# GpSimd's maxima and masks also wait for VectorE's last listed operation on two SBUF operands, in a listed order searched anew

## The chip, the core and the metric

The kernel runs on one core of a Trainium2 chip. The metric is the device time of one execution in microseconds: 606.67 us for the kernel before, the median of 3 runs (606.17 to 608.17). The five engines of the core take their instructions in the order in which the program gives them and run beside each other; semaphores order them where data passes between them. In the profile they are PE (TensorE), DVE (VectorE), ACT (ScalarE), POOL (GpSimd) and SP (SyncE, which here only issues DMAs).

## The reference, cut to what matters

Two stages follow each other for 8 batches of 576 positions. The first is linear attention with 8 heads of 64 values:

```python
def phi(x):
    proj = x @ w_phi                                  # 64 -> 128
    proj = proj - max(abs(proj), over the 128)
    return concat([exp(proj), exp(-proj)])            # 256 features
kv = phi(k).T @ v ;  z = sum over s of phi(k)
attn = (phi(q) @ kv) / (phi(q) @ z + 1e-6)
```

The second takes the 512 values of a position as x and mixes 4 experts, of which each position uses the 2 with the largest gate. Every expert is a causal softmax attention over the 576 positions with its own weights:

```python
logits = x @ w_gate;  w = softmax over the 2 largest
scores = 0.125 * (x @ wq[e]) @ (x @ wk[e]).T, causal
a = softmax(scores);  out += mask * w * (a @ (x @ wv[e]) @ wo[e])
```

All data is float32.

## The kernel before

The work is cut into 32 pairs of heads (p) for the first stage and 8 batches of 2 expert groups (n = 0 to 15) for the second; keys lie on partitions and positions along the free dimension or the other way round, as the products need it.

*First stage.* `stream_k` projects the keys of a pair (L485), `center` takes the largest absolute value of each row (L548) and subtracts it (L551), `phi_k` takes the two exponentials on ScalarE. For 28 of the 32 pairs `key_sum` adds one half of ek to zs with an accumulating DMA that GpSimd issues (`add_to`, L318), and VectorE closes the sum with one addition in SBUF (L560); TensorE then multiplies zs with ones (L621) among the products of phi(k) and v (L610). `stream_q` projects the queries (L485). For them the largest value runs across partitions, so `phi_q` has GpSimd do a PARTITION_ALL_REDUCE of u into mx (L680, 64 of them), VectorE subtracts mx from u (L682), and ScalarE takes the exponentials. `stream_n` multiplies (L707 for the denominator, L718 for the numerator), `divide` applies the reciprocals and splits the result into a high and a low float32r part (x, L751 and L285).

*Second stage.* `stream_b` projects x to q, k and v (L281), splits q and k into two parts (ql at L791, kkl at L285) and makes the scores (L838). `evac_s` copies them to the tile s in SBUF. `mask` has GpSimd set what lies behind the diagonal to a very small number (AFFINE_SELECT, L946, 80 of them). `maxima` gathers, key block by key block, the largest score of each column on VectorE (L959), has GpSimd reduce it across partitions (PARTITION_ALL_REDUCE of top into max, L963, 16 of them), and subtracts it from the scores on VectorE (L967: for each group five operations, for 1152, 896, 640, 384 and 128 elements). `expo` takes the exponentials, `add_up` sums them over key blocks (L979), `sums` sums them over partitions with ones (L1005), `attend` multiplies by v (L1034), `evac_y` scales and splits the result (yl, L285), and `out_unit` makes the output product (L281). `gates` works out the two chosen experts per position in a row of small VectorE operations (L901 to L919).

*The order of the work.* Each of these functions is a stream that yields a `Step` for every piece of work. The string ORDER (3,100 characters) is a list made by an offline search: each character names the stream that goes on next, by its place among the streams alive. The string SIDES (520 digits) settles for each copy that ScalarE or VectorE could do which of them does it (0 ScalarE, 1 VectorE). The instructions of each engine come into the program in the order of that list, and `in_order` ties each instruction to the one before it on the same engine, so that each engine keeps it. Between different engines only the data's own dependencies order anything. The class `Plan` accounts for costs while the list is worked off: `run` for an engine's instruction, `transfer` for a DMA, with GpSimd's recent instructions (`pool`, and how long each of them keeps VectorE's two-operand work out: `blocked`) and VectorE's latest operation of that kind (`shared`). These figures drive the search; they put nothing into the program.

Of the kernel before, what the change touches and what calls it, by code (L numbers as in the profile page):

```python
# [11 lines left out]
AF = mybir.ActivationFunctionType  # L12
ALU = mybir.AluOpType
# [4 lines left out]
DM, E = 512, 4  # L18
# [35 lines left out]
KVD = 6  # L54
RATE = 2.18
TRATE = 2.4
ADD_RATE = 40.0
EXIT = 95.0
ENTRY = {'F': 102.0, 'R': 99.0, 'S': -31.0, 'C': 23.0, 'Q': 10.0}
LDW = 109.0  # L60
# [4 lines left out]
def change_cost(a, b):  # L65
# [4 lines left out]


ORDER = (
    r'41000000008BB40929DEB742BC6BD9E9I88IDD1C007000=0CDBDHBD55342BEH=GG::99=BCBEBCBFDECD2E==CDB:BB478=>0DEED546EFE='
    r'BD0=79EEE9::IID=I8F8DBH:EDE>2>ID>HB9HGI3BDB9=5=1EJHF2HJH:7:DACBFF8IHIG<B0:;;H:F@A3<549<FFGD<BE;9EEHGBEE:D6E:CF'
    r'7DF88:FD3H71?2@:F:G?;;::CAH?BBB:G;G9C9CF88AH43G0G@568=83EB>DHI10DKLHD8>A==H94HGEFA897G7CF9@B8D0CB6A@8DHC5BB?IA'
    r'>=6AI;=F2;8;:;@;>8KKG?BDA=GH=G;FA;88C@DD8DB8C=;6AAFG5G9G=A9GEEGE9BAG77DBACGF;G;HB@8E;;MDO6808803IIJJFJIAH>EF;>'
    r'D48F;;;F>CA;HHEAFFE8=E6FFE@8@A8A;;5??B>:LABGGG>@@@@@H@DF=A1::::KIBHEG:@AE>?DB:999OHKE@LKMKCCLF338LL>?B28882088'
    r'88D678>IBEIG5BFEE?>79ID==93884889@KKCLJ66L02GCIE?88JCC@77DH=?99G88=DD1GAEAAD<8259<7HKH=7@FKG238808KK<HEK8F=86D'
    r'MNJMHI<E?DFJD8=G997EH=DA=<=I<H7:=KK:HH:G:H:F<KK<EEL<J::8II;IL;MLJALHKI::DAFIMF=8?FKF@?:8A8:>:HFF8K83B2H84MO5PG'
    r':LG6RCI=@E::DJHGIH::;IF>EF>FDK@?>DIHDIB=GCDDEE;;B>88DE:>CE@=FF85<AADHAG<K<<CKCAC>FIAAAI=GJH@<?FFIDDH?DJ@C=C::H'  # L80
    r'J=FJI=E@G?:9LFCC@<KI@KK999KEEC88B;>@H?8>>>CC@CAB?F?FBEBFDA3881ICDDD?BB6;;<B?D>70072B8FECBDD88>A>89B>9A=G>8>=78'
    r'L78KEEL586;9CKCMMQCOPCHKOOKLLE<998B@30I78I9DHGJ8FGG@HE6E5EA88>?41G28AI=88II7FKE?C::::K::86:BAKJ8EIAA?C6JKCKJCG'
    r'DF4F=89FFF8F89A3<87::BGBB?D78DC2GB@1JD??FG::F5?DG?CBHK::J=LB:J?>=NGKJD:8:>IH;BED8IB>>F=C;C82CBIG=C8DBFG8D9BDD8'
    r'CD?F:::G::@=JBFOAGBIQ=BQBBFJHOC<<I<D<NEJQLJLCDEK<D99KA9I=CEA0888383BD@@>G@LFAJKEJAGCEDH@<JEIF77HD6JKI9IID9CDF7'
    r'E5F?EBCHII6D87FIIHHFG0C8B<EDA888GEE48?<>@@===G=HB08659M8KPJLLGNKMD8M98;9J;L<MILL;8H986JL6ALKGIFIGI22F@HF5:8IHI'
    r'<1GHF<E<08<888077:::DF:FIAIO:PI>?=>FNCKJGL33828K9JEJ98G87IIJEDCIK:7J8IJ8H::H@I:OQDJJL:6:;LF5NMCI8B?83OCOQOCB::'
    r'B:@SHJCMI>FMB8K=J0AII:JAAJG==LK?H;8D=>F=;:IHCECG6GD89G88F<DIHEG<:::HIHJ=J5>:JB<CS@@EBBKAKEBIIJ<<9ARI6Q@Q9B9488'
    r'8138MD7N=EF<0828FLFCOJ<FLLHK8L88MKICCCJK9@9F94LK88888M87==IJ@JD7JJ?=HF>B2EGCJI<99EFA67I9IJCMLI??H@GEF88F6H?D5E'
    r'757HHJDAFEMFFFEAGAA:E:::<:IE=AJLEL:A896KLIJE8828833019=JAHD77D??HGC8=AAGIID8GJHHI86=DH;5<K8GMBNJLL=M<<A===NNJC'
    r'3JK@088<<<<FH:;;NQIMNHINOHHK42881K08::HH8MLF?MJIMAG:EH:;EG>PG66EBKRHNL:::H:PF:OMLJG8NO@GBHGIL?GIFCH8GF:;;F=>AF'  # L90
    r'D<>:EHFD:5ELKHFEEBHF::=L=9LPC>PPFCDD<DID<;TCQBBOQJIM<<<BPK@PJDAA9<BHIJOO9M<JMEJ9JNO@P@@8KN882FG=<KLJBD88GKI8IE'
    r'D88GDEIE@G?C70EDC8GF?576JF9D4?E?IJ9D9?K>@@HGGBFHI3HFG03888821887@C>@7;;M>D=<68GC6B?EHDBB8FF?E99G95E82B>8ED>C<E'
    r'<BF7F78388IJCI8CB@B:68::<KKCIDAA@:::JFHBJCABC8FHHFCF9895BEFEEB88D7:DDIED19H9HLD;99:J9GNJ=A>B6FJ?G70=;D;QHLG1JG'
    r'NMGF9F9JCII990@2IED7HC>JC=G7I5JCG7G@CHH<DF7::4;<HEJ=F9EHH@EAB;;;EE7FE;;D;=GFCG;;8@>FE5>>>AHFIG99DCFNGLCGH9@@>E'
    r'>239CO@@@:BTCSDBIFK<B?GI=@MD8887PDEA7J7L6O67BBEAKA?HACGHIE>JI06JBB>6<CD>66B=BE6>?B43>7=:<7EF2BEB5055516C;GCF;F'
    r'D<G;FA88CDF6F6HH0CG@AC884@44CC2@4?4<8;5>@3DDB>>@>>3966331>26H69:6>C<445K242@I1?3<G?A1F1H@1<@FE1ED3;@3=31A>B85@'
    r'B;8C:33E23GF2?15@>>A61=;9C6=<<;>;6?73?3>??1::>;61008228;>8;??=0>>;=7671>;=;:8;7;833<<<449<44>>>65:42<484227445'
    r'84484?0101170=95B=52;A@07649??2=:><?@?440404FD355>:?05=;A4<65<5900480474<5<6:657::48:008:297769387477742263209'
    r'000023320110::42849::2666964800790<09;79767=7069;59:0:907887887:878:50::788651017611562006605850580==;444:9<1;'
    r'6711;17<7139=68259984455456461345111111341413585112111411;3:2=32998818810081124465454452330000>>?256028=1<<15;'  # L100
    r'32056538645204042200'
)

SIDES = (
    r'11000001001100010000100000000011000000000111000000011010000001000001110100000100000000010000000000000000000000'
    r'00000000000000000000000010000000000100000001000000000000010000001100100001000000110000001010000010000000000100'
    r'00000000001000010000100110000001000000000001001000010010010000000010010000000000000001000000000001010001001110'
    r'01000000000101000001000100000010100000000010000000010000011100000000100000000010000000001000100011001000100111'
    r'00000000001000000000001000011000000110000100000111000000000000010000000001000110'
)  # L110


# [6 lines left out]
class Plan:  # L119
# [16 lines left out]

    def clocked(self, t, cost, rows):
# [19 lines left out]
    def run(self, eng, cost, w=(), r=(), rows=128, tiling=(128, 128), port=False):  # L157
        if eng == 'PE' and tiling != self.tiling:
            cost += change_cost(self.tiling, tiling)
        if eng == 'PE':  # L160
            self.tiling = tiling
        t = self.free.get(eng, 0.0)
        for k in r:
            t = max(t, self.after(self.ready, k, eng))
        for k in w:
            t = max(t, self.after(self.last, k, eng))
        if eng == 'PE':
            cost = self.clocked(t, cost, rows)
# [12 lines left out]
        for k in w:
            self.ready[k] = self.last[k] = (end, eng)

    def transfer(self, cost, issue, w, r, eng='SP'):
# [6 lines left out]
        self.free[eng] = t + issue  # L191
        ring = int(eng == 'POOL')
        self.rings[ring] = max(self.rings[ring], t + issue + 650.0) + cost
        end = self.rings[ring] + 1150.0
        for k in r:
            if end >= self.last.get(k, (0.0, 'SP'))[0]:
                self.last[k] = (end, 'SP')
# [43 lines left out]

def in_order(tc):

    last = {}
    for i in tc.nc.cur_bb.bb.instructions:
        if i.engine in last:
            tc.add_manual_dep(i, last[i.engine].name, mybir.DependencyInfo(
                mybir.DependencyClass.NoSync, mybir.DependencyReason.DATA), reason="order")
        last[i.engine] = i


@with_exitstack
def tile_linear_attn_moe(ctx, tc, qt, kt, v, wts, out):
# [643 lines left out]
    def gates(b):  # L897
# [14 lines left out]
        yield Step('ACT')
        act(20, ex, ex, [G], [], AF.Exp)
# [245 lines left out]
```

## Time and profile before

| | before |
|---|---|
| median of 3 runs | 606.67 us (606.17 to 608.17) |
| the profiled execution, own time | 607.85 us |
| its span, first to last instruction | 605.8 us |
| mean granted TensorE clock | 0.999 of full speed |
| DMA | 67.13 MB, mean 111 GB/s |

The span is what the profile covers, from the first to the last instruction of the core; the execution's own time has what lies around it as well. In the rows below an engine is busy while one of its instructions runs. A row of groups gives a line of the program, engine and operation, tiles written and read, shape, count, busy time and the mean time of one instruction, then the time for which the engine sat idle before these instructions and what ended it. A row of the timeline gives the start, the time covered, and the instruction; neighbours of one line are merged (x2 means two instructions, and the shape shown is that of the first). Of matmuls the ends are modelled, and spans on POOL are rough.

### The profile page before, as it was taken

The numbers are of one execution on the slowest core, as the hardware profiler recorded it, in microseconds if no ns is written. First come the engines' busy times: TensorE is split into PE (matmuls) and PEld (weight loads), VectorE is DVE, ScalarE is ACT, GpSimd is POOL, SyncE is SP. The second block draws the span as 40 slices with busy tenths as digits, with TensorE's granted clock in tenths as the row PEclk, the third lists the DMA queues.
The fourth block names the chain that finished last, engine by engine and source line by source line (L and its number), as shares of the span: only waits on it lengthen the run. The fifth ranks groups of instructions, "written<-read, shape, count | busy, mean of one in ns | idle before, by whom it ended". The sixth has DMA issues, their size and how long they took to land.

```text
span 605.8 us, 19534 instructions
## 1 busy us (share of the span) xinstructions
PE 582.0 (96%) x7909; PEld 447.9 (74%) x7909; DVE 553.5 (91%) x1172; ACT 449.2 (74%) x1087; POOL 275.1 (45%) x195
## 2 busy tenths in 40 slices
PE   8998999998999999999999999998999999999986
PEld 6664788566885788767885877965888677778975
DVE  6897899999999999998989999999999989998994
ACT  3998877867796878866879668866778768675653
POOL 3754553366615554346542663316743449231420
PEclk9999999999999999999999999999999999999999
DMA  8556465650436562465535544446434542221012
GB/s 217 162 152 133 102 144 124 143 125 26 101 88 148 126 172 68 106 148 135 146 83 128 137 120 116 98 131 149 103 102 100 117 94 83 37 68 40 1 49 110
DMA packets 55369, 67.13 MB, mean 111 GB/s; under 512 B 23664, under 2 KB 31216, under 8 KB 55280
## 3 DMA queue, kind: packets, MB, share of 16 engines
q1 hardware_dynamic: 47344, 50.62, 29.1%
q0 software_dynamic: 7616, 14.68, 14.8%
q8 instruction: 62, 1.02, 0.7%
q10 hardware_dynamic: 320, 0.59, 0.4%
q14 instruction: 27, 0.22, 0.1%
HBM read 36.64 MB, written 14.55 MB: 85 GB/s over the span
## 4 chain that ended last, share of the span: by engine, by line
PE 63%; DVE 18%; DMA 7%; ACT 5%; issue 4%; POOL 2%; SPq 1%; DVEq 0%; POOLq 0%; ACTq 0%
PE ps_c L281 26%; PE ps_c L485 7%; PE ps_c L718 6%; PE ps_c L838 6%; PE ps_c L610 5%; PE ps_c L1034 5%; DMA zs<-ek 5%; PE ps_c L707 4%; DVE s L967 3%; DVE top L959 2%; ACT ek L292 1%; PE ps_c L621 1%; DVE u L682 1%; DMA q_in<-in_qt_dram 1%; DVE max L979 1%
## 5 line engine op out<-in xcount | busy, mean ns | idle before, releaser
L680 POOL PARTITION_ALL_REDUCE mx<-u x64 | 146.0, 2319 | 45.2 <-ACT u L290 22.9
L281 PE MATMUL ps_c<-x,qk 128*128 128x256 f32 (+1 forms) x768 | 106.6, 298 | 0.0
L281 PEld LDWEIGHTS ps_c<-x,qk 128*128 128x128 f32 x768 | 102.4, 189 | 4.4 <-ACT u L290 1.0
L946 POOL TENSOR_SCALAR_AFFINE_SELECT s<-s 128x256 f32<-128x256 f32 (+1 forms) x80 | 44.2, 597 | 108.7 <-ACT s L290 87.1
L963 POOL PARTITION_ALL_REDUCE max<-top x16 | 57.5, 3595 | 58.7 <-DVE top L959 28.9
L318 POOL DMA_DIRECT2D zs<-ek x28 | 34.2, 1223 | 94.4 <-ACT ek L292 65.7
L967 DVE TENSOR_TENSOR s<-s,max 128x1152 f32<-128x1152 f32 (+4 forms) x80 | 73.2, 944 | 0.0
L292 ACT ACTIVATE ek<-ek 128x1024 f32<-128x1024 f32 x64 | 67.7, 1058 | 3.6 <-DVE ek L551 2.8
L292 ACT ACTIVATE s<-s 128x1152 f32<-128x1152 f32 (+4 forms) x80 | 57.5, 741 | 10.5 <-DVE s L967 10.2
L610 PE MATMUL ps_c<-ek,v_in 128*32 128x256 f32 x1024 | 61.7, 381 | 0.5 <-ACT ek L292 0.5
L290 ACT COPY s<-ps_c 128x512 f32<-128x512 f32 (+4 forms) x129 | 48.0, 427 | 11.6 <-PE ps_c L838 11.1
L281 PE MATMUL ps_c<-yh,wo 128*128 128x256 f32 (+1 forms) x256 | 52.7, 300 | 0.0
L682 DVE TENSOR_TENSOR u<-u,mx 128x576 f32<-128x576 f32 x64 | 51.6, 816 | 0.2 <-POOL mx L680 0.2
L290 ACT COPY u<-ps_c 128x320 f32<-128x320 f32 (+1 forms) x107 | 40.1, 402 | 12.7 <-PE ps_c L485 11.9
L281 PE MATMUL ps_c<-vg,x 128*128 128x260 f32 x384 | 49.1, 285 | 0.0
L1034 PE MATMUL ps_c<-s,vs 128*32 128x320 f32 (+4 forms) x896 | 46.5, 357 | 2.0 <-DVE ql L791 2.0
L281 PEld LDWEIGHTS ps_c<-vg,x 128*128 128x128 f32 x384 | 47.1, 188 | 0.8 <-issue 0.2
L610 PEld LDWEIGHTS ps_c<-ek,v_in 128*32 128x32 f32 x1024 | 31.4, 110 | 21.8 <-issue 2.7
L292 ACT ACTIVATE mx<-u 128x576 f32<-128x576 f32 x64 | 42.9, 682 | 5.8 <-DVE u L682 5.5
L548 DVE TENSOR_REDUCE pmax<-ps_c 128x4 f32<-128x512 f32 x64 | 42.7, 680 | 2.7 <-PE ps_c L485 2.5
L485 PE MATMUL ps_c<-q_in,wf 64*128 64x256 f32 (+1 forms) x256 | 43.5, 442 | 1.1 <-DVE ek L551 1.0
L1034 PEld LDWEIGHTS ps_c<-s,vs 128*32 128x32 f32 x896 | 28.1, 110 | 21.4 <-DVE ql L791 2.3
(131 smaller groups left out, 1357.9 us busy)
## 6 DMA issues: line engine op xcount, KB each, us to landing
zs<-ek POOLq DMA_DIRECT2D x28, 512.0 KB, 6.2
out_dram<-ot SPq DMA_DIRECT2D x32, 288.0 KB, 2.2
q_in<-in_qt_dram SPq DMA_DIRECT2D x60, 144.0 KB, 4.1
k_in<-in_kt_dram SPq DMA_DIRECT2D x64, 128.0 KB, 3.7
v_in<-in_v_dram SPq DMA_DIRECT2D x32, 256.0 KB, 3.2
kvd<-kvt SPq DMA_DIRECT2D x104, 48.0 KB, 2.2
kv<-kvd SPq DMA_DIRECT2D x26, 192.0 KB, 2.8
vt_in<-in_v_dram SPq DMA_DIRECT2D x16, 128.0 KB, 3.3
```

What stands on the lines that cost most here:

```text
L281: nc.tensor.matmul(o, a, b, start=start, stop=stop, skip_group_check=True)
L290: nc.scalar.copy(o, i)
L292: nc.scalar.activation(o, i, func, **kw)
L485: nc.tensor.matmul(o, a, b, start=True, stop=True, skip_group_check=True)
L548: dve(512, [mk], [pk]).tensor_reduce(out=m[:, us], in_=src, axis=AX.X, op=ALU.max, apply_absolute_value=True)
L610: nc.tensor.matmul(o[g, 0:2], v_in[:, 4 * h + t, k:64:2], ek[:, :, 2 * TURN[t] + h, :].rearrange("p c (w f) -> p c w f", w=4), start=False ...
L680: nc.gpsimd.partition_all_reduce(M, U, 128, bass_isa.ReduceOp.absmax)
L682: dve(S, [uk], [mk], port=True).tensor_tensor(out=U, in0=U, in1=M, op=ALU.subtract)
L946: nc.gpsimd.affine_select(out=d, in_=d, pattern=[[0, 2], [1, w]], compare_op=ALU.is_ge, fill=FILL, base=0, channel_multiplier=-1)
L963: nc.gpsimd.partition_all_reduce(big.rearrange("p e s -> p (e s)"), top.rearrange("p e s -> p (e s)"), 128, bass_isa.ReduceOp.max)
L967: dve(2 * (S - 128 * j), [('d', x, j)], [('max', z)], 1.11, True).tensor_tensor(out=block(s_, j, None, rows(j)), in0=block(s_, j, None, ro ...
L1034: nc.tensor.matmul(ps[r:r + 32, q0 - s0:s1 - s0], vs[:, j, 128 * g + 64 * e + k:128 * g + 64 * e + 64:2], ss[x][:, e, o + q0:o + s1], star ...
```

## The change

Three things are changed. `in_order` gives each of GpSimd's all-reduces and masks one more dependency with a semaphore: on the last VectorE instruction that stands before it in the list and reads two operands from SBUF (or copies from SBUF); operations with an operand in PSUM (tiles named ps_) do not count. GpSimd's DMA issues and memsets get no such wait. The planner is told of that wait (`pairs`), of the measured issue time of GpSimd's DMAs, another rate and landing time, and of the port flag of five small gate operations. And ORDER and SIDES are replaced as a whole: the lengths are the same, 3,100 and 520; SIDES had 93 ones and has 76.

```diff
-ADD_RATE = 40.0
+ADD_RATE = 45.0
...
 ORDER = (
...
 SIDES = (
...
         if eng == 'DVE' and port:
             cost += self.blocked(t)
             self.shared = (t, t + cost)
+            self.pairs = t + cost
+        if eng == 'POOL' and port:
+            t = max(t, self.pairs + 215.0)
         if eng == 'POOL' and self.shared[0] < t < self.shared[1]:
             t = self.shared[1]
...
-        end = self.rings[ring] + 1150.0
+        end = self.rings[ring] + (1500.0 if ring else 1150.0)
...
 def in_order(tc):
 
-    last = {}
+    def two_from_sbuf(i):
+        names = [x.bass_ap.tensor.name for x in i.ins if hasattr(x, 'bass_ap')]
+        least = 1 if isinstance(i, mybir.InstTensorCopy) else 2
+        return len(names) >= least and not any(n.startswith('ps_') for n in names)
+
+    last, pairs = {}, None
     for i in tc.nc.cur_bb.bb.instructions:
...
         last[i.engine] = i
+        if i.engine == mybir.EngineType.DVE and two_from_sbuf(i):
+            pairs = i
+        elif pairs is not None and type(i).__name__ in ('InstPartitionAllReduce', 'InstTensorScalarAffineSelect'):
+            tc.add_manual_dep(i, pairs.name, mybir.DependencyInfo(
+                mybir.DependencyClass.Sync, mybir.DependencyReason.DATA), reason="order")
...
-    def add_to(o, i, w, r):
-        plan.transfer(o.free_size() * 128 / ADD_RATE, 1000, [w], list(r), 'POOL')
+    def add_to(o, i, w, r, issue=1220):
+        plan.transfer(o.free_size() * 128 / ADD_RATE, issue, [w], list(r), 'POOL')
...
-        dve(80, [G], []).tensor_tensor(out=ge, in0=ge, in1=tri.unsqueeze(1).to_broadcast(sh4), op=ALU.mult)
+        dve(80, [G], [], port=True).tensor_tensor(out=ge, in0=ge, in1=tri.unsqueeze(1).to_broadcast(sh4), op=ALU.mult)
```

## Rows read from the trace of the kernel before

**Rows 1.** Page, parts 1 and 4: busy us (share) xinstructions; the chain by engine.

```profile
PE 582.0 (96%) x7909; PEld 447.9 (74%) x7909; DVE 553.5 (91%) x1172; ACT 449.2 (74%) x1087; POOL 275.1 (45%) x195
...
PE 63%; DVE 18%; DMA 7%; ACT 5%; issue 4%; POOL 2%; SPq 1%; DVEq 0%; POOLq 0%; ACTq 0%
```

**Rows 2.** Stretches: from:to and length, busy us by engine, PEclk, DMA share, GB/s.

```profile
20.00:580.00 560.00, 545.80 (x7456) 418.62 (x7453) 523.58 (x1091) 427.05 (x1039) 263.20 (x186) 1.00 0.45 109
580.00:606.00 26.00, 18.58 (x248) 16.05 (x246) 16.88 (x39) 11.49 (x31) 2.88 (x1) 0.98 0.24 92
```

**Rows 3.** Waits of PE alone: us in total, times, longest us.

```profile
PE ps_c L621 <- DVE zs L560: 5.6, 4, 2.3
PE ps_c L707 <- DVE x L285: 2.5, 2, 1.3
```

**Rows 4.** Groups of DVE by shape: xcount | busy us, mean ns | idle before, releaser.

```profile
L682 DVE TENSOR_TENSOR u<-u,mx 128x576 f32<-128x576 f32 x64 | 51.6, 816 | 0.2 <-POOL mx L680 0.2
...
L967 DVE TENSOR_TENSOR s<-s,max 128x1152 f32<-128x1152 f32 x16 | 24.7, 1545 | 0.0
...
L560 DVE TENSOR_TENSOR zs<-zs 128x512 f32<-128x512 f32 x28 | 21.4, 764 | 9.2 <-DMA zs<-ek 9.1
L959 DVE TENSOR_TENSOR top<-s 128x896 f32<-128x896 f32 x16 | 20.1, 1259 | 0.9 <-POOL s L946 0.8
...
L979 DVE TENSOR_TENSOR max<-s 128x896 f32<-128x896 f32 x16 | 17.3, 1078 | 1.0 <-ACT s L292 0.7
...
L979 DVE TENSOR_TENSOR max<-max,s 128x384 f32<-128x384 f32 x16 | 8.9, 558 | 0.3
...
L979 DVE TENSOR_TENSOR max<-max,s 64x128 f32<-64x128 f32 x16 | 4.4, 273 | 0.3
```

**Rows 5.** Timeline, 132 to 142 us: start us, us, engine line, [idle before <-releaser].

```profile
132.76 9.10 POOL L680 PARTITION_ALL_REDUCE mx<-u  x4
132.95 4.49 DVE L967 TENSOR_TENSOR s<-s,max 128x1152 f32<-128x1152 f32 x2
...
141.37 0.86 PE L1034 MATMUL ps_c<-s,vs 128*32 128x256 f32 x16 [2.03 <-DVE ql L791]
```

**Rows 6.** Timeline, 192 to 196 us.

```profile
192.19 2.81 DVE L967 TENSOR_TENSOR s<-s,max 128x384 f32<-128x384 f32 x2
...
193.11 4.72 POOL L680 PARTITION_ALL_REDUCE mx<-u  x2
...
195.45 0.69 PE L707 MATMUL ps_c<-mx,kv 128*32 128x288 f32 x8 [1.25 <-DVE x L285]
```

**Rows 7.** Timeline, 412 to 417 us.

```profile
412.61 3.59 POOL L963 PARTITION_ALL_REDUCE max<-top  x1 [4.51 <-DVE top L959]
...
413.27 2.00 DVE L560 TENSOR_TENSOR zs<-zs 128x512 f32<-128x512 f32 x1 [0.85 <-DMA zs<-ek]
...
415.32 0.43 PE L621 MATMUL ps_c<-zs,ones 128*32 128x128 f32 x8 [1.59 <-DVE zs L560]
```

**Rows 8.** Timeline, 577 to 583 us.

```profile
579.21 3.67 POOL L963 PARTITION_ALL_REDUCE max<-top  x1 [4.47 <-DVE ge L901]
...
579.95 1.49 DVE L907 TENSOR_TENSOR gt<-gt 128x20 f32<-128x20 f32 x1
581.47 0.18 DVE L908 TENSOR_TENSOR gt<-gt,cnt 128x20 f32<-128x20 f32 x1
...
582.41 0.41 PE L281 MATMUL ps_c<-yl,wo 128*128 128x320 f32 x1 [2.01 <-DVE yl L285]
```

**Rows 9.** Groups of POOL by shape, columns as in rows 4.

```profile
L680 POOL PARTITION_ALL_REDUCE mx<-u x64 | 146.0, 2319 | 45.2 <-ACT u L290 22.9 <-DVE u L302 13.0 <-DVE pmt L537 7.4
L963 POOL PARTITION_ALL_REDUCE max<-top x16 | 57.5, 3595 | 58.7 <-DVE top L959 28.9 <-DVE zs L560 8.3 <-DVE ge L901 4.5
```

**Rows 10.** Copies out of PSUM on DVE, by shape, columns as in rows 4.

```profile
L302 DVE COPY u<-ps_c 128x256 f32<-128x256 f32 x12 | 4.9, 415 | 1.2 <-PE ps_c L485 0.9
```

**Rows 11.** Copies out of PSUM on ACT, by shape, columns as in rows 4.

```profile
L290 ACT COPY u<-ps_c 128x256 f32<-128x256 f32 x52 | 18.4, 372 | 6.8 <-PE ps_c L485 6.6
```

More of the change, by code (lines that the diff above doesn't have):

```diff
@@ L72 @@
 ORDER = (
[L73 to L101, printed above, removed]
+    r'10000030084C0009CD9247DC26FBGB98BB0935E708GFG=HDB84DCH010HKDJGGHB0G0BG2EE=990=CBI5=BBD=7B::JE>2DHCC:4463=7988B'
@@ new lines @@
+    r'B=GGBJDD9::EGEE=>ELD=IH5:>21BJJEDE>HGD99=CCGHICFEB=G7J:H:ABH5425468FJ<IIE<0A<C;E@<<BFDGGF@EA;6DEEBFD@D7A;0HDE7'
+    r'7JEDEDG6H9;;D99B8:F@B979G9C>AGFE99808E17A:?2AF@59H3CIJ6CEFB99LCL0IHFFJFG::H4>>>>96877D9FJ=EB8@FBBIBB=GBGB>8B6?'
+    r'>EA;;5;;FGF;JDD@EAF?88E3=F012;C88:ECEDD8@6;5;=>B=?B8BBB999AEDID7BA6EBD=IHDA7;GH8DFC@;;;6IDJ;@H;HMJIHHB;EG;CCB?'
+    r'FFFFGCFB18H08038F48G88;5HAGFAA=;;:CL>?8CCECBAAKCBB@:::B:9AGJC<EHG99HFF=A?DDDIEJ@BCC883228888D::I6P88GFKHINBF83'
+    r'NGMA@77?NA5FE31?I@CKFD<99>>9KK<=KAKC8884820HKEKFI=E8GHA6=<DE987FF>B976G7>7I88I=<E=DAHD2<88888=5J9GALC<032KHBBJ'
@@ new lines @@
+    r'HA8?6L<LK0IKGBAF899=@77=H==BKDA:::<JJIOF>:N<<DIFAIIH::CLMDIIKH8;HEJJ;CEH:CI:LGC6;GF8H:IL5FKG8:::KGL@OQPN88IO::'
+    r':MMM?J=M:A>L>AIK4MMKIKFFF?J882K>IJ=JE0IEE;G;HF<DE<<G?FHFGF=F@IC<:8M8;:5BGGIDHHCDFJEE<8IICHIC=BLIKMDHMC::JPOI:9'
+    r'MPO<GRHHBFFPPP999JH6<D18EEGAF8J>FC<7F0CEIE@D38DFD83@@KCC@I>GG8BBHF;;BIH<E7C>CFG2DE8BBD?C==8DC>88B>==9;9=97KI7L'
+    r'JI=F=FF8B5OG68OEOGB>E8888KLA9BL9M79F?LAGIKM8JJ54IJAIHJ8H6H<38=1@82887?G=BFB::::EJ6F:MDK=DEFAK:J<?F@8806C@??ACD'
+    r'FF:AFGF988897GF?DAEDA>CDC7@@GDE2:G:C5KG:B@DCB8M@:J=EOA::N:088834230?IFHJFJI@I:IF=:H?GG=I=ABECD;98I88;EGH6E=AGG'
@@ new lines @@
+    r'EBED8D6C::DC::HCC:EDLGGIMMM<CDJ<@<KBBS=<<O?DNA9AFKRDOC;HEG99JDCBFJ?GAABI<K=J?883E??EG?E7GFF@GHG@FB@F79F=9H1ACM'
+    r'CAGG<E5D888HAG2CAFF7I7888=@3>IDFF8D<E<8EEF<8<BCE<>G56889M>PQ8DCJHN8K>LLK>HK99;D9;IJ0JGHJD8GI@GG?EEEGF8E577:HK<'
+    r'FFE<FH6FE>0::::8D88142C8M6EC?<CDEDG@K::FLHDA8893IBF@9EJFJ8AHE>D8FF87HF7I:CGJFDGDB:L::K:5LHJFAAGQ6@I>GF8JF=MMHI'
+    r'K>A88D:EE:JE=AAF;:08==EI@D@@CGC8<ECGG8;;9JG8EE8DH:CIFFE>=H><G:<:5BEH:DCGF:>O6OE:<<HB2HGD@ANK<9A=KO@IP<M06GO93C'
+    r'A1842883MF9EDBMHM888>88MIIH8KEK>AG9989IG=A8FJH8K7F78LL7L6HH8C>PHIQ=NHGCFKF23AKG8999NIE;H?K7B<HH5B=7IAHEEMJG4EI'
@@ new lines @@
+    r'I708IAE@:GG>DB<D8FB:B::NNG66:KFLL::K3@B8210828588KH9BJJILI=CABD9G78GJ7IJ6AF=B8HJ8LAMFGGLH=5<K<KJA8J==L=JA==E<D'
+    r'DQIHO83880<P<<<;NHS;:BSHHGN8O8HMKN8NHHA:>:D:G=KGPFOB?OO:OKHLLIGGA:@NG:::;8<EKGNM6I?>MJKH>?FF;6K=IIIHGF;:FGFF8:'
+    r'=I:9LCKEAB::FKLLFCD5JTE<RRRIDLFD<ETB<QQ10C4<DCNDCHEGCGC=MJCD<0QLQMHBF@EHCJ@9FE<9823GD88F@@I@HCC@GB88E<E888BECD'
+    r'?HB;98HC<><>7@EBFABF5F76FEEELHF99481H@EIH>J@>@@DGHH9J6@FC6IF;;77KHN<LIH83J8888GEF989<HF8F<288@839@GG@HFCFH077K'
+    r'JBI>CA28A<H858CCC<68:II::B:NELHHIJIACCHID:6IICE:89HE98FF5HC?GFGF@BFFGF7=::KJJG::M::LIKELPHH7H8F<FCNC<<>OOGOO0H'
@@ new lines @@
+    r'GFHJ:::;8:8F?J8?@MJ??KL>DDDH2=38GJGCDFDFF;;88;5FFH8<HKLKBHCB>CC6<EF<=@@DFDCH<C<BB:=??D?9EDFFFCJF::?FJGHEIIHH:G'
+    r':AAEPG9NUD=NF9=C?FKF9G7QPD1737016NPMJNPDOPN?AF?77ICCE>?LDD16055GI5?J9H;<<?=AB5@<=A=AE3<2<E?666555GF=FD<50DHI:G'
+    r'C<G;E;FE:9851?BB7558D?D@A54A2>AB@A4??4A3C12?A?>=2C==2C244EE6<222D654446I@BEH4=>=CF0007607020=CFDCD?0224459:=<0'
+    r'B22A9=H112>I>@AF<ID080=C224C220@E9@>?0B88577<06:?7<:>59<:19::69:>99B?=8A9:2>3=0>:395;<:<7:9777445444085?=>=0<<'
+    r'2<52;>7C6C99916@611000022?0@?87559A3A=5?3@C8=58:84:;;00<656670=888?6@88<7>;;=7=9:0;;6<<03<<9628488366442223:30'
@@ L102 @@
+    r'0000052258;;5:<32811:78:7796301000:2997:0>@55855509896598001005:7:;68757577;57515766655315005005846440:3B5@;5?'
+    r'3;:=<1:8751715::2146464755444151211411143463311048518832223=;63229883717100817555667055651210010<=413<<<0<00::'
+    r'52912855552200543010'
 )
 SIDES = (
-    r'11000001001100010000100000000011000000000111000000011010000001000001110100000100000000010000000000000000000000'
-    r'00000000000000000000000010000000000100000001000000000000010000001100100001000000110000001010000010000000000100'
@@ L107 @@
-    r'00000000001000010000100110000001000000000001001000010010010000000010010000000000000001000000000001010001001110'
-    r'01000000000101000001000100000010100000000010000000010000011100000000100000000010000000001000100011001000100111'
-    r'00000000001000000000001000011000000110000100000111000000000000010000000001000110'
+    r'10000000111000000000000011000010000011000011000000010000000000000100100100000001000000000010000000000000000000'
+    r'00000000010000001100000100000000000000000000000000000000000000000100001001000000000000110000000000000000000000'
@@ L110 @@
+    r'00001000000000000000010100000010100010000100000101000000110000000100000000000000010000001000010000000001000000'
+    r'00010010110000000000101001000000000000000000000000010000001000110000000000011000000000011100000000100110101010'
+    r'00100000100000000000000011000000000000010000000100000000001000000000000010110101'
 )
@@ L134, in __init__ @@
         self.shared = (0.0, 0.0)
+        self.pairs = 0.0
         self.done = set()
@@ L906, in gates @@
         dve(80, [G], []).tensor_reduce(out=lost, in_=ge.rearrange("p t a b -> p t b a"), axis=AX.X, op=ALU.add)
-        dve(20, [G], []).tensor_tensor(out=lost, in0=lost, in1=won, op=ALU.subtract)
-        dve(20, [G], []).tensor_tensor(out=lost, in0=lost, in1=cnt, op=ALU.add)
+        dve(20, [G], [], port=True).tensor_tensor(out=lost, in0=lost, in1=won, op=ALU.subtract)
+        dve(20, [G], [], port=True).tensor_tensor(out=lost, in0=lost, in1=cnt, op=ALU.add)
         dve(20, [G], []).tensor_reduce(out=gs[:, 0], in_=lg, axis=AX.X, op=ALU.max)
-        dve(20, [G], []).tensor_tensor(out=ex, in0=lg, in1=gs[:, 0].unsqueeze(2).to_broadcast([128, 5, 4]),
+        dve(20, [G], [], port=True).tensor_tensor(out=ex, in0=lg, in1=gs[:, 0].unsqueeze(2).to_broadcast([128, 5, 4]),
                                        op=ALU.subtract)
@@ L918, in gates @@
         dve(5, [G], [], 8.0).reciprocal(gs[:, 1], gs[:, 1])
-        dve(20, [G], []).tensor_tensor(out=gw[:, 0:20].rearrange("p (e j) -> p j e", j=5), in0=w,
+        dve(20, [G], [], port=True).tensor_tensor(out=gw[:, 0:20].rearrange("p (e j) -> p j e", j=5), in0=w,
                                        in1=gs[:, 1].unsqueeze(2).to_broadcast([128, 5, 4]), op=ALU.mult)
```

## The prediction, made before the changed kernel ran

> **What bounds the kernel now.** I read the page's busy times first, then the stretches, then TensorE's waits, and only then GpSimd and VectorE. TensorE (PE) is busy for 582.0 of 605.8 us, VectorE (DVE) for 553.5, ScalarE (ACT) for 449.2, GpSimd (POOL) for 275.1 [rows 1]. So PE is the bound and 23.8 us of the span is its idle time. Of that, 7.4 us lies in the last stretch (26.00 − 18.58) and 14.2 us between 20 and 580 us (560.00 − 545.80) [rows 2]. The first thing to see is therefore a ceiling: what makes PE's waits vanish in the long middle stretch can win 14 us, 2.3%, and no more. The chain that ended last goes through DVE for 18% and ACT for 5% [rows 1]: where PE waits, it mostly waits for DVE. PE's own waits name it: for the add that closes the key sums (zs, L560) 5.6 us in four pieces, for x (L285) 2.5 us in two [rows 3]; two waits of 2.0 us, for ql and for yl, follow below.
>
> Why is DVE late just there? An operation on two SBUF operands beside GpSimd's work takes longer than the same operation alone. The max-accumulation at L979 gives the undisturbed price: 1078 ns for 896 elements and 558 for 384, so 1.016 ns an element, hence 1338 ns for 1152, 753 for 576 and 688 for 512. Against that L967 with 1152 elements has a mean of 1545, L682 one of 816, L959 with 896 one of 1259, L560 one of 764 [rows 4]. The overruns are 16 x 0.207 = 3.3 us, 64 x 0.063 = 4.0, 16 x 0.181 = 2.9 and 28 x 0.076 = 2.1: 12.3 us in these four forms, not spread evenly but in a few large collisions. Four of them can be followed to PE:
>
> - At 132.95 two subtractions of L967 (1152 and 896 elements, the loop's first two) take 4.49 us where 1.34 + 1.08 are usual, beside four all-reduces from 132.76 on; PE then waits 2.03 us at 141.37 [rows 5].
> - At 192.19 the last two (usual 0.56 + 0.27 [rows 4]) take 2.81 us, and two all-reduces begin at 193.11, in the middle of them; PE waits 1.25 us at 195.45 [rows 6].
> - At 413.27 L560 takes 2.00 us in place of 0.69. An all-reduce of the maxima had begun 0.66 us before. PE waits 1.59 us [rows 7].
> - At 579.95 an operation on 20 elements takes 1.49 us where its neighbour of the same size takes 0.18; the last all-reduce of the maxima had begun 0.74 us before. PE waits 2.01 us [rows 8].
>
> **The change, part by part.** *The wait.* 160 instructions of GpSimd (64 + 16 all-reduces, 80 masks) now also wait for the last DVE operation on two SBUF operands that stands before them in the list. In all four places above a GpSimd instruction was under way beside the DVE operation, in three of them it had started first. Where the list has the DVE operation ahead, the wait turns this round: DVE runs at its usual price and GpSimd starts after it. What can come back is the smaller of overrun and PE wait: 2.03 (overrun 4.49 − 1.34 − 1.08 = 2.07), 1.25 (2.81 − 0.56 − 0.27 = 1.98), 1.31 and 1.31, together 5.9 us. An operation listed behind a GpSimd instruction can still run into it, and which pairs stand that way round in the new list no row tells. The bounds are 0 (all four collisions come again elsewhere) and 5.9. I take three of four, 4.4 us: nearer to the upper end, since an all-reduce can no longer run freely ahead of the list as the four from 132.76 on did.
>
> *What the wait holds up.* GpSimd works in order. Behind a held all-reduce stand the next masks and the 28 accumulating DMAs for zs (L318); behind these stands L560, and behind that PE at L621. Today DVE's L682 waits 0.2 us in all for its 64 all-reduces [rows 4], so the cover is complete: GpSimd is idle for 605.8 − 275.1 = 330.7 us [rows 1] and its results come early. The trace has no such wait, so I bound it: below 0 (this slack covers all), above as much again as PE's whole wait at L621, 5.6 us [rows 3]. I take 1.0, nearer to the row of L682. Without the slack, every late all-reduce would cost DVE up to its 2.3 us (3.6 for the maxima) [rows 9].
>
> *Evacuations.* The list of sides has 520 decisions, of which 93 named DVE and 76 do now. Seventeen copies out of PSUM leave DVE (0.415 us for 256 columns) for ACT (0.372) [rows 10, 11]: DVE −7.1 us, ACT +6.3 us. By their shares of the chain [rows 1] that is 0.18 x 7.1 = 1.3 us won and 0.05 x 6.3 = 0.3 lost: 1.0 us won, an estimate. If ACT's extra work fell on the chain by DVE's share it would be about nothing; if every copy that goes had held PE up, 7.1. I take 1.0, as the chain has the shares now.
>
> *The new order.* Both lists have 3,100 steps and the work is the same. In characters 300 to 2,500 the marks 5 to 9, : and ; (the long-lived streams, which give PE most of its work) alternate 191 times in both; so I leave PE's 582.0 us as they are, and keep 3 us either way for the range. The planner's constants (DMA rate, issue, landing, port flags on small gate operations) put no instruction on the chip; they act through the order alone.
>
> **The sum.** 4.4 + 1.0 − 1.0 = 4.4 us won. The profiled execution took 607.85 us for a span of 605.8; it stands 1.18 us above the median of 606.67. I carry the difference over to the median: 602.3 us.
>
> **Rivals.**
>
> 1. *Held too long (slower).* GpSimd now goes in step with DVE and no longer ahead of it. If zs and the maxima come late, PE's waits at L621 double (+5.6) while the collisions only move, and the copies give back 1.0: 606.67 + 5.6 − 1.0 = 611.3. It decides as soon as the holds cost PE more than about 5.4 us, all that the other two terms bring. For it: an all-reduce of 2.3 us sits between a hold and its consumer, and the zs DMAs are in the same queue. Against: DVE's wait of 0.2 us today, and the 330.7 us of idle time.
> 2. *Nothing comes of it.* The new order meets other collisions of the same size, the more so as the change's wait does not cover the DVE operations listed behind a GpSimd instruction: with 1.0 won by the copies and 1.0 lost by holds, 606.7. For it: the planner also counted blocked DVE operations before, and the trace is full of them all the same. The change would then do what its words say but not what removes the overruns.
> 3. *Each collision is dearer than its row shows.* At 413.27 L560 was done 2.66 us after the all-reduce began and its own work takes 0.69, so it was let in 1.97 us into an all-reduce of 3.59 [rows 7]. If in other places DVE has to stay out until the end, it would be 2.93 us in place of 1.31, 2.2 times; with 2.2 x 4.4 = 9.7 us won the time would be 597.0. The Trainium skill (SBUF — State Buffer, section on the two separate sides) has this rule: whichever of the two starts first holds the shared port pair for its whole instruction. The row disagrees, so its chance is small.
>
> **How the numbers follow.** A difference of 0.3%, 1.8 us, is about what a measurement of this kernel can tell from no change; faster means below 604.8, slower above 608.5. The forecast has 0.55: the overruns are large, they stand right ahead of PE's waits, and the wait acts on just these. Its own range is 598.5 (all four places, no holds, 1.3 us from copies: 606.67 − 5.9 − 1.3 is 599.5, a little under that with the order's part) to 604.8. Rival 1 has 0.22, rival 2 0.18, rival 3 0.05. Faster 0.60, same 0.18, slower 0.22. For the range I go down to 595.5 (599.5 less the 3 us for PE's order, less 1 us), which leaves out nearly nothing, and up to 609.5, inside rival 1, which leaves out about 0.17.
>
> **What would show it.** Right: the means of L967, L959, L682 and L560 come down to the prices worked out from L979; DVE's busy time falls by more than the 7 us of the copies; PE's single waits of over 1 us become fewer; GpSimd's idle time is ended by L682, L967, L959 and L979 in many places. Wrong: DVE's L682 or L959 wait for GpSimd by several us, or L560 for its DMA, and PE at L621 for more than 5.6 us (rival 1); or the overruns stay near 12 us (rival 2); or PE's busy time itself moves by more than 3 us, in which case the order and not the wait has decided.

## The result, and the profile after

The changed kernel takes 600.01 us, the median of 6 runs (597.77 to 601.02), against 607.25 us for the kernel before beside it: a ratio of 0.9859, with a 95% interval of 0.9832 to 0.9886 (the quotient of the two medians, 0.988, lies inside it). By the medians that is 7.2 us shorter, where 4.4 had been forecast. The profiled execution has a span of 598.2 us (605.8 before).

Busy times and the chain that ended last, page of the changed kernel; they answer to [rows 1]:

```profile
PE 582.6 (97%) x7909; PEld 448.3 (75%) x7909; DVE 542.5 (91%) x1155; ACT 452.0 (76%) x1104; POOL 276.9 (46%) x195
...
PE 75%; DVE 14%; ACT 4%; DMA 3%; issue 2%; POOL 1%; SPq 1%; ACTq 0%; DVEq 0%; POOLq 0%
```

PE's work is what it was (582.6 us, 582.0 before), so what the span lost is idle time of PE: 605.8 − 582.0 = 23.8 us before, 598.2 − 582.6 = 15.6 us now. DVE is busy for 11.0 us less and its share of the chain falls from 18% to 14%. Where PE's idle time went is seen in the same two stretches as [rows 2]:

```profile
20.00:580.00 560.00, 552.06 (x7538) 424.81 (x7538) 518.49 (x1085) 435.20 (x1066) 268.55 (x187) 1.00 0.45 110
580.00:599.00 19.00, 12.42 (x160) 10.18 (x152) 10.29 (x23) 6.49 (x20) 0.00 (x0) 0.97 0.29 110
```

In the long middle stretch PE is idle for 560.00 − 552.06 = 7.9 us in place of 14.2, so 6.3 of the 8.2 us are from there. The stretch at the end, counted to the end of each span, gave 1.4 us (5.8 in place of 7.2; the prediction's 7.4 runs 0.2 us past the span), the first 20 us the rest. PE's waits, with the same columns as [rows 3]:

```profile
PE ps_c L635 <- DVE zs L574: 1.8, 1, 1.8
PE ps_c L1019 <- DVE max L993: 1.5, 2, 1.2
PE ps_c L295 <- DVE ek L565: 1.3, 1, 1.3
...
PE ps_c L852 <- DVE yl L299: 1.0, 1, 1.0
```

L635 is L621 of before: its four waits of 5.6 us in all have become one of 1.8. The wait of 2.0 us for ql has gone to 0.2, and for yl there is one of 1.0 in place of 2.0. Why, is in DVE's groups, which answer to [rows 4] (L696, L981, L574 and L973 are L682, L967, L560 and L959 of before):

```profile
L696 DVE TENSOR_TENSOR u<-u,mx 128x576 f32<-128x576 f32 x64 | 50.0, 793 | 0.0
...
L981 DVE TENSOR_TENSOR s<-s,max 128x1152 f32<-128x1152 f32 x16 | 23.1, 1443 | 1.5 <-POOL max L977 1.4
L574 DVE TENSOR_TENSOR zs<-zs 128x512 f32<-128x512 f32 x28 | 20.1, 716 | 0.1
...
L973 DVE TENSOR_TENSOR top<-s 128x896 f32<-128x896 f32 x16 | 17.8, 1113 | 3.3 <-ACT s L304 3.0 <-POOL s L960 0.3
...
L993 DVE TENSOR_TENSOR max<-max,s 128x384 f32<-128x384 f32 x16 | 9.9, 622 | 0.4
```

With the prediction's prices (753, 1338, 688 and 1078 ns) the overruns are 64 x 0.040 + 16 x 0.105 + 28 x 0.028 + 16 x 0.035 = 5.6 us, where they were 12.3. Not all of that went away: L993 is L979 of before, the group that gave the undisturbed price, and its 384 elements now take 622 ns in place of 558. Over all forms I count an operation on SBUF operands as overrun when it takes over 0.09 us more than the median of its own form; that gives 24.4 us in 35 operations before and 16.5 us in 31 now. So the collisions are somewhat fewer and above all shorter, but they are not gone. This total is used below for every run.

The wait itself can be seen where the loop of L981 runs, as in [rows 5]:

```profile
126.98 2.32 DVE L981 TENSOR_TENSOR s<-s,max 128x1152 f32<-128x1152 f32 x2
...
128.39 2.91 POOL L694 PARTITION_ALL_REDUCE mx<-u  x1 [1.01 <-DVE s L981]
...
129.62 1.98 DVE L981 TENSOR_TENSOR s<-s,max 128x640 f32<-128x640 f32 x2
```

The first two subtractions take 2.32 us, the usual 1.34 + 1.08 less their overlap. GpSimd sat idle for 1.01 us until DVE released it, and its all-reduce begins at 128.39, 0.07 us after the usual end of the first subtraction (126.98 + 1.34 = 128.32). The second one is already under way by then and keeps its time; the all-reduce takes 2.91 us where the mean is 2.34. The third comes in the middle of it and is kept out: the third and fourth take 1.98 us where the kernel's own rows have 0.82 for 640 elements (558 + 256 x 1.016) and 0.56 for 384. An operation listed behind the all-reduce is what the wait doesn't touch.

One cost in this trace is not one of GpSimd's. After PE's wait of 1.82 us, which ends at 295.99, the clock granted to TensorE is at half (1.2 of 2.4 GHz) for one stretch:

```profile
297.60:301.00 3.40, 3.40 (x17) 3.40 (x16) 3.15 (x9) 2.81 (x10) 2.31 (x1) 0.50 0.21 54
```

Its price is worked out with the experiments below (1.5 us).

### The profile page after: what moved, and what is told of

Same layout as the page of the kernel before. It is cut to its first block, busy times and chain, and to the rows that moved or that the text cites. A ratio compares the mean times of both kernels' runs of the same rounds, so it can differ in the third digit from the quotient of the medians.

```text
span 598.2 us, 19532 instructions
## 1 busy us (share of the span) xinstructions
PE 582.6 (97%) x7909; PEld 448.3 (75%) x7909; DVE 542.5 (91%) x1155; ACT 452.0 (76%) x1104; POOL 276.9 (46%) x195
## 4 chain that ended last, share of the span: by engine, by line
PE 75%; DVE 14%; ACT 4%; DMA 3%; issue 2%; POOL 1%; SPq 1%; ACTq 0%; DVEq 0%; POOLq 0%
PE ps_c L295 28%; PE ps_c L499 11%; PE ps_c L732 9%; PE ps_c L624 7%; PE ps_c L852 5%; PE ps_c L721 4%; PE ps_c L1048 4%; DVE s L981 2%; DVE top L973 2%; DVE max L993 2%; PE ps_c L591 1%; PE ps_c L635 1%; DMA q_in<-in_qt_dram 1%; DVE pmax L562 1%; DVE u L696 1%
## 5 line engine op out<-in xcount | busy, mean ns | idle before, releaser
L694 POOL PARTITION_ALL_REDUCE mx<-u x64 | 147.5, 2336 | 71.8 <-ACT u L304 14.2
L960 POOL TENSOR_SCALAR_AFFINE_SELECT s<-s 128x256 f32<-128x256 f32 (+1 forms) x80 | 42.5, 562 | 94.3 <-ACT s L304 17.9
L977 POOL PARTITION_ALL_REDUCE max<-top x16 | 57.4, 3590 | 56.2 <-DVE top L973 19.3
L332 POOL DMA_DIRECT2D zs<-ek x28 | 34.3, 1224 | 75.5 <-DVE pmax L562 15.6
L981 DVE TENSOR_TENSOR s<-s,max 128x1152 f32<-128x1152 f32 (+4 forms) x80 | 66.6, 867 | 1.5 <-POOL max L977 1.4
L306 ACT ACTIVATE s<-s 128x640 f32<-128x640 f32 (+4 forms) x80 | 57.2, 739 | 6.4 <-DVE s L981 6.1
L304 ACT COPY s<-ps_c 128x320 f32<-128x320 f32 (+4 forms) x140 | 52.6, 432 | 10.9 <-PE ps_c L852 10.2
L295 PE MATMUL ps_c<-yh,wo 128*128 128x320 f32 (+1 forms) x256 | 52.9, 300 | 0.0
L696 DVE TENSOR_TENSOR u<-u,mx 128x576 f32<-128x576 f32 x64 | 50.0, 793 | 0.0
L732 PE MATMUL ps_c<-mx,kv 128*32 128x320 f32 (+1 forms) x512 | 43.4, 410 | 0.5 <-ACT u L304 0.3
```

The source lines that it names most:

```text
L295: nc.tensor.matmul(o, a, b, start=start, stop=stop, skip_group_check=True)
L304: nc.scalar.copy(o, i)
L306: nc.scalar.activation(o, i, func, **kw)
L694: nc.gpsimd.partition_all_reduce(M, U, 128, bass_isa.ReduceOp.absmax)
L696: dve(S, [uk], [mk], port=True).tensor_tensor(out=U, in0=U, in1=M, op=ALU.subtract)
L732: nc.tensor.matmul(ps[g:g + 32, 0:n], kvi[:, 2 * k + (h ^ p % 2), 32 * c:32 * c + 32], P_[h][c][:, s0:s1], start=c == 0, stop=c == 1, skip ...
```

## The experiments

Each run stands beside the kernel before on the same chip. Overruns are counted as above.

| run | what it is | us | ratio to before, 95% | overruns us |
|---|---|---|---|---|
| changed kernel | new list, wait on all 160 | 600.0 | 0.986 (0.983 to 0.989) | 16.5 |
| e1_wait_only | list of before, wait on all 160 | 661.8 | 1.091 (1.088 to 1.094) | 16.7 |
| e2_order_only | new list, no wait | 618.7 | 1.019 (1.017 to 1.022) | 49.0 |
| e3_reduces_wait | new list, wait on all-reduces | 597.9 | 0.984 (0.982 to 0.986) | 19.3 |
| e4_masks_wait | new list, wait on masks | 617.6 | 1.016 (1.014 to 1.019) | 40.8 |
| after_again | the changed kernel again | 599.4 | 0.986 (0.983 to 0.989) | 16.4 |
| e5_sides | 17 more copies on DVE | 608.0 | 1.002 (1.000 to 1.004) | 14.8 |
| e6_later | all-reduces 0.3 us later | 596.2 | 0.982 (0.979 to 0.984) | 12.1 |
| e7_other_ops | wait for the other DVE operations | 634.1 | 1.044 (1.042 to 1.047) | 36.1 |
| e8_before_sides | before, 17 copies to ACT | 611.7 | 1.007 (1.004 to 1.010) | 23.3 |
| e9_pinned | before, 25 chosen waits | 601.2 | 0.989 (0.986 to 0.992) | 12.4 |
| e10_fills_twice | all-reduces 0.75 us later | 609.4 | 1.003 (1.001 to 1.005) | 20.5 |
| e11_reduces_fills | e3 and e6 together | 598.3 | 0.984 (0.980 to 0.987) | 15.0 |

### The wait without the list, and the list without the wait

The wait alone puts the changed `in_order` into the kernel before:

```diff
 # kernel before, list and sides unchanged
+        elif pairs is not None and type(i).__name__ in ('InstPartitionAllReduce', 'InstTensorScalarAffineSelect'):
+            tc.add_manual_dep(i, pairs.name, ...)
```

> The list of before with the new wait alone (600.0 us is the changed kernel, 607.2 the one before). Theory W (the wait brings the gain by itself, since it lets VectorE's two-operand work go first): VectorE's overruns fall well below the 24 us before, and the time goes to 600 to 604 us. Theory O (the gain is the new order's; a list that was made without the wait has GpSimd's instructions in places where they are held for many microseconds): the overruns fall all the same, but VectorE now waits for all-reduces by 10 us or more, and the time is above 607, up to 625 us. Theory B (both are needed): as O here, and the new list without the wait is at 604 us or more.

It took 661.8 us, 55 us more than the kernel before: worse than Theory O's bound. The overruns fell to 16.7 us as all theories had it. What was paid for that is in the waits (who waited for whom, total, times, longest):

```profile
DVE zs L570 <- DMA zs<-ek: 32.7, 16, 4.4
PE ps_c L631 <- DVE zs L570: 31.6, 12, 6.7
...
DVE u L692 <- POOL mx L690: 22.5, 12, 3.5
```

PE waits at L631 (L621 of before) 31.6 us in 12 pieces for the zs sum, which waits 32.7 us for its DMAs, which GpSimd issues behind held all-reduces. And L692 (L682 of before) waits 22.5 us for all-reduces, where it had been 0.2 [rows 4]. In all PE is idle for 60.2 us (659.6 of span less 599.4 busy) in place of 23.8. The other 17.4 us are PE's own work, 599.4 us in place of 582.0: the granted clock is at half in six stretches, 31 us together, and 0.975 in the mean. So idle time is about two thirds of the loss, and the rest goes with the lower clock. The list of before had never said where an all-reduce stands among DVE's operations, since nothing between engines hung on it. In the trace of before 92 of the 160 instructions began before the end of the operation for which they would now wait, some by 16 us.

The other half takes the wait out of the changed kernel:

```diff
 # changed kernel, list and sides unchanged: in_order as before
-            tc.add_manual_dep(i, pairs.name, ...)
```

> The new list and sides without the wait. Theory W: the overruns of VectorE come back to about 24 us and the time to 605 to 608 us. Theory O: 599 to 601 us, overruns at the 16.5 us of the changed kernel or a little above. Theory B: in between and above 603 us, with GpSimd again starting ahead of VectorE's operations.

It took 618.7 us, 12 us more than the kernel before and longer than any of the three theories had it, with 49.0 us of overruns in 62 operations. Theory B is the one that stands: neither half, as it is, brings anything without the other. DVE's groups show it:

```profile
L686 DVE TENSOR_TENSOR u<-u,mx 128x576 f32<-128x576 f32 x64 | 57.0, 903 | 0.0
...
L745 DVE TENSOR_TENSOR facy<-facy,gc 128x18 f32<-128x18 f32 x16 | 12.7, 792 | 0.2
```

L686 (L682 of before) has a mean of 903 ns in place of 793. The product on 18 elements at L745 takes 792 ns, and in the timeline there is why:

```profile
414.12 3.58 POOL L967 PARTITION_ALL_REDUCE max<-top  x1 [1.06 <-DVE facy L742]
414.12 2.13 DVE L745 TENSOR_TENSOR facy<-facy,gc 128x18 f32<-128x18 f32 x1
...
416.17 0.68 DVE L555 TENSOR_TENSOR ek<-ps_c,pmax 128x512 f32<-128x512 f32 x1
```

An operation of 0.17 us that begins together with an all-reduce of the maxima is kept for 2.13 us. Without the wait, 84 of the 160 instructions begin before the end of the operation for which they would wait, by 7.7 us at most. Why the new list then has more collisions than the old one is not shown; it was searched with the wait in the plan.

### Which waits carry it

```diff
 # changed kernel
-        ... type(i).__name__ in ('InstPartitionAllReduce', 'InstTensorScalarAffineSelect'):
+        ... type(i).__name__ in ('InstPartitionAllReduce',):               # e3
+        ... type(i).__name__ in ('InstTensorScalarAffineSelect',):         # e4
```

> The changed kernel with the wait on the 80 all-reduces alone; the 80 masks are free again. An all-reduce keeps VectorE out for 1.2 to 2 us, a mask for 0.2 to 0.4. If the wait's gain is that of collisions with all-reduces: 600 us, within 1 us of the changed kernel, overruns up by 1 to 2 us. If the masks' part matters: 602 us or more.

> The changed kernel with the wait on the 80 masks alone; the all-reduces are free again. If the wait's gain is that of collisions with all-reduces: the same time as the new list without any wait, within 1 us. If masks carry it: 600 us.

The all-reduces carry all of it: with their wait alone 597.9 us, 2 us less than I had expected, and with the masks' alone 617.6, within 1.1 us of no wait at all (618.7). The 80 waits of the masks remove 2.8 us of overruns (19.3 to 16.5) and bring no time.

### Is it the two-operand work, or only the step?

```diff
 # changed kernel
-        if i.engine == mybir.EngineType.DVE and two_from_sbuf(i):
+        if i.engine == mybir.EngineType.DVE and not two_from_sbuf(i):
             pairs = i
```

> The changed kernel with GpSimd's 160 instructions waiting for the last listed VectorE operation that does NOT read two SBUF operands (with an operand in PSUM, a transpose, a reduction), in place of the last that does. If what counts is that GpSimd and two-operand work keep out of each other's way: overruns between the changed kernel's 16.5 us and the 49 us of the new list without a wait, and a time of 604 to 616 us. If what counts is only that GpSimd goes in step with VectorE, whatever it waits for: 599 to 602 us.

Overruns of 36.1 us, between the two as expected, so what GpSimd waits for does count. The time of 634.1 us lies outside both of the ranges expected: these waits also hold GpSimd at places for which the list was not made. L981 (L967 of before) waits 15.4 us for the maxima, L696 10.2 us for its all-reduces.

### The overruns alone, with the list of before

To price the overruns without a new list I took 25 collisions of the trace of before, in each of which the DVE operation stood ahead of the GpSimd instruction in the list, and let that instruction wait for that operation alone:

```diff
 # kernel before, list and sides unchanged; PIN: GpSimd's instruction -> the operation it ran into
+            if n in PIN:
+                tc.add_manual_dep(i, pairs[PIN[n]].name, ...)
```

> The kernel before, its list and sides unchanged, with 25 single waits: each GpSimd instruction that collided in the trace of before with a VectorE operation listed ahead of it waits for just that operation (holds of 0.5 to 5 us, against up to 16 us with the wait as the change has it). These collisions had 21.1 of the 24.4 us of overruns. If removing overruns is by itself worth what the prediction counted (4.4 us, at most 5.9 at the four places): 601 to 604 us, with overruns of 3 to 10 us. If the overruns only move, or the holds eat the gain: 606 us or more, with overruns of 15 us or more or VectorE waiting for GpSimd by several us.

601.2 us, 6.1 us less than the kernel before (607.2), with overruns down from 24.4 to 12.4 us (3 to 10 had been expected). This is the prediction's mechanism by itself, though not its sum: between the two traces the same matmul starts earlier by 2.4 us more across 130 to 142 us of the trace before, by 1.3 across 193 to 196 and by 1.5 across 413 to 417, 5.2 us at the places of [rows 5], [rows 6] and [rows 7], for which the prediction had 4.6. Other places that it had not followed bring 4.4 us more. From 580 us on 1.9 us are lost again: the fourth place [rows 8] did not pay, and shows what such a wait can't do:

```profile
570.36 0.18 DVE L922 TENSOR_TENSOR gt<-gt 128x20 f32<-128x20 f32 x1
...
570.74 3.58 POOL L978 PARTITION_ALL_REDUCE max<-top  x1 [5.62 <-DVE gt L922]
570.87 2.01 DVE L925 TENSOR_TENSOR gt<-vs,gs 128x20 f32<-128x20 f32 x1
...
573.33 0.64 PE L296 MATMUL ps_c<-yl,wo 128*128 128x320 f32 x1 [2.57 <-DVE yl L300]
```

The all-reduce now waits for the 20-element product at 570.36, begins 0.20 us after its end, and meets the third operation behind that one instead: 2.01 us in place of 0.18, and PE waits 2.57 us, more than before. The granted clock is at half there, from 572.89 to 576.31.

### How much slack the holds have

Two fills of an unused tile (64 elements) behind the wait and ahead of each all-reduce make it start some 0.3 us later (0.34 from the first fill's start to its own, median):

```diff
 # changed kernel; the fills wait as the all-reduces do
+        nc.gpsimd.memset(junk, 0.0)
+        nc.gpsimd.memset(junk, 0.0)
         nc.gpsimd.partition_all_reduce(...)
```

> The changed kernel once more, so that the others of this call have it on the same chip: 599 to 601 us.

> The changed kernel with two small fills of an unused tile (64 elements on 128 partitions, an estimated 0.3 us together from fills of 128 and 260 elements that took 0.20 and 0.31) ahead of each of the 80 all-reduces, behind the same wait, so that each held all-reduce starts some 0.3 us later. If GpSimd's idle time covers the holds, as the prediction has it: at most 1 us longer. If the new list has the results come just in time: 3 us or more longer, with VectorE waiting for all-reduces or for the zs DMAs.

The changed kernel took 599.4 us and the one with the fills 596.2: no longer, even shorter. The slack covers 0.3 us. Where the 3 us come from can be told in part. Across the stretch at 297 to 301 us, in which the changed kernel had half the clock, e6 gains 1.5 us on it: the matmuls at L635 start 1.09 us later in e6, those at L852 behind the stretch 0.41 us earlier. That is the price of that stretch; in e3, too, the gain there is 1.5 us. A row of e3 for it, beside the one of the changed kernel above (17 matmuls in 3.40 us there, 29 here):

```profile
297.60:301.00 3.40, 3.40 (x29) 3.35 (x27) 3.40 (x8) 2.99 (x10) 2.21 (x1) 1.00 0.23 61
```

The times bear this out: of the twelve executions of the changed kernel, the six with a mean clock of 0.999 or more took 598.2 us in the mean and the six at 0.996 or 0.997 took 600.4, and e6 stayed at 0.998 or more in all four. The overruns are fewer, too (12.1 us); what they bring here was not measured apart. With four fills, about 0.75 us:

> The changed kernel with four of the small fills ahead of each all-reduce in place of two, about 0.6 us. With two it took 596.2 us against 599.4 without. If a later start of the all-reduces is good by itself (less of it meets VectorE's next operation): 596 us or less and overruns below 12 us. If the two fills were only a lucky shift: 597 us or more. If the slack ends: 600 us or more, with VectorE waiting for all-reduces.

609.4 us: a further 0.4 us costs some 13 us, and the gain is gone. Who waited for whom says by what:

```profile
DVE u L701 <- POOL mx L699: 5.3, 4, 2.0
...
DVE s L990 <- POOL max L986: 4.6, 8, 1.6
```

L701 (L682 of before) waits for its all-reduces, L990 (L967) for the maxima, 9.9 us together. The slack ends between 0.3 and 0.75 us. The last run puts the two shorter variants together:

> The changed kernel with the wait on all-reduces alone and two fills ahead of each: the two variants that were shorter than the changed kernel (597.9 and 596.2 us) put together. If their gains add up: 594 to 595.5 us. If both only missed the stretch of half clock near 298 us in the changed kernel: 596 to 598 us.

598.3 us, between the changed kernel and e6, so the gains don't add up. Its profiled execution keeps the full clock at 297 us and has a span of 594.1 us like that of e6, and yet its median is 2 us longer than e6's. The clock goes with this as well: the three executions at 0.996 took 598.7 to 599.3 us, the three at 0.998 or more 595.8 to 597.9. Of the variants that beat both kernels, e6 with 596.2 us is the shortest, but its interval touches that of the changed kernel, so a real lead over it is likely rather than shown; what else separates these variants from each other is left open.

### The copies

```diff
 # e5: changed kernel, 17 zeros of SIDES made ones, evenly spread (76 -> 93)
 # e8: kernel before, 17 ones of SIDES made zeros, evenly spread (93 -> 76)
```

> The changed kernel with 17 copies out of PSUM, spread evenly over the list, given back from ScalarE to VectorE (93 of 520 on VectorE, as before). The prediction's sum had 1.0 us for them. If that is right: 0.5 to 2 us longer than the changed kernel. If the copies lie beside other work: the same within 0.5 us. If VectorE is the engine that everything waits for: up to 7 us longer.

> The kernel before with 17 of its 93 copies on VectorE, spread evenly, moved to ScalarE (76 remain, as in the changed kernel), and no wait. If VectorE's load by itself carries a large part of the gain: 3 to 7 us shorter than the kernel before. If the copies stand where each list has them for a reason: the same within 1 us, or longer.

Giving DVE 17 copies more costs the changed kernel 8.7 us, above the 7 that I had put as the most; taking 17 from DVE makes the kernel before 4.5 us longer. In both directions a change of sides without a new search loses. These runs don't undo the change's own choice: copy by copy, the two kernels differ in 135, 76 of which went from DVE to ACT and 59 from ACT to DVE, and 17 is only the balance. Other picks of 17 were not tried. In e5's profile PE is late at one place above all, and what follows is dearer than the wait:

```profile
555.00:559.00 4.00, 2.37 (x37) 2.03 (x34) 3.50 (x5) 2.44 (x7) 0.78 (x2) 1.00 0.41 152
559.00:566.00 7.00, 6.39 (x31) 5.72 (x32) 3.75 (x9) 1.51 (x6) 1.64 (x4) 0.51 0.00 0
```

PE has 1.6 us without work before 559 us and the granted clock is 0.51 for the 7 us that follow. This execution is the longest of e5's twelve (611.75 us at a mean clock of 0.992); the others had 0.994 to 0.998, so this place explains only part of the 8.7 us.

## Why the prediction was right, and where its terms were not

**The bound and the place** hold. PE's work did not move, and 6.3 us of the gain are PE's idle time in the middle stretch, where it waited for DVE behind collisions with GpSimd.

**The wait (4.4 us, bounds 0 and 5.9).** Right in kind, a little small: the 25 chosen waits of e9 brought 6.1 us with the list of before. Three of four places paid, as it had assumed, 5.2 us; the fourth stayed, since there another operation took the blow. That the total is near 5.9 is in part chance, since 4.4 us from places outside the sum met 1.9 us lost at the end. All-reduces alone carry it, masks do not, which the prediction had not told apart.

**The holds (1.0 us lost, bounds 0 and 5.6).** For the new list nothing speaks against the value: DVE waits 1.4 us for the maxima (L981 above), and a start 0.3 us later costs nothing; no run prices the holds there by themselves. The upper bound was far too low as a statement on the wait: with the list of before the kernel is 55 us longer, ten times that bound, and 31.6 us of PE's waits are in just the queue that the prediction named (all-reduce, zs DMA, L560, PE at L621). The bound was read from a trace in which GpSimd ran free, and with that list 330.7 us of idle time were no cover: 92 instructions had begun ahead of the operation's end. The cover left now is thin, under 0.75 us.

**The copies (1.0 us won, from their share of the chain).** This step failed. It priced 17 copies that leave DVE, where 76 left and 59 came, and the chain's shares did not price even an evenly spread 17: one way they cost 8.7 us in one list, the other way 4.5 in the other. What the change's own sides are worth by themselves no run shows.

**The order (0, with 3 us either way).** Not neutral either: without the wait the new list, with its sides, is 12 us longer than the old one. That the two lists alternate equally often (295 and 294 changes among these marks, not 191) said nothing on where GpSimd's instructions stand.

So the mechanism was right, and that the sum came near the result is in part luck. Its terms don't add up one by one: the wait alone measures 55 us lost, list and sides alone 12 lost, both together 7.2 won. The copies and the holds, +1.0 and −1.0, cancelled in the sum without either having been borne out. Rival 1 (held too long) was real, and the list is what kept it out; rival 2 (the collisions only move) is half true, 16.5 of 24.4 us remain. Rival 3 is answered below.

## What to carry to other kernels

Where two engines get in each other's way, an order between them can be worth more than more freedom. Imposed everywhere it paid here only in the list that was made with it, while 25 chosen waits paid in the old list as it stood: test the wait and the list apart before either is given the credit. Price a hold by how far the held instructions run ahead of what they will wait for (92 of 160 here, by up to 16 us), and not by the idle time of their engine or by the 0.2 us for which a consumer waits while nothing is held. A single trace was enough to pick the places where a wait pays: 25 waits brought most of what 160 waits and a new search did.

## What the runs showed of the hardware

An all-reduce keeps a two-operand operation of DVE out for a part of its time only. In 17 collisions of five traces (before, changed, e2, e4, e7) with an all-reduce of the maxima alone, DVE was let in 1.95 to 2.24 us after its start (median 1.96) while it ran for 3.58 to 3.86; that is DVE's end less its usual time less the start of the all-reduce. The Trainium skill (SBUF — State Buffer, section on the two separate sides) says that the one that starts first holds the port pair for its whole instruction; by that it would have been 3.59, and the measurement decides. The smaller all-reduces (576 elements) do the same: in 96 collisions of these traces DVE was let in 0.96 to 1.00 us before such a one ended, whether it ran for 2.13 or for 3.60 us. In none of these was DVE kept out to the end, which answers rival 3. Issuing an accumulating DMA from GpSimd alone kept DVE's operation out too, until 0.37 to 0.49 us after the start of an issue of 1.22 us (4 cases). Larger collisions can follow such an issue: in the trace before, the second subtraction of [rows 6] begins at 192.65, 0.46 us ahead of the all-reduce, and is kept out all the same; a DMA issue had begun at 192.34. Three more collisions there (112.70, 125.00 and 358.92) are like this, and in all four DVE was let in 2.35 to 2.38 us after the start of the issue.

TensorE's clock fell to half after single waits of some 2 us in some executions and not in others with the same wait: in the changed kernel after 1.82 us that ended at 295.99, at the same matmul in e3 not after 1.81 us and in e6 not after 2.16, with no difference that I could find ahead of it. That stretch of 3.4 us cost 1.5 us.
